# Loading four weight halves instead of two ahead of a loop that runs zero times, in an attention, experts and dense kernel

## The chip, the cores and the metric

The kernel runs on one core of a Trainium2 chip. Its engines are TensorE (PE; its weight loads are PEld), VectorE (DVE), ScalarE (ACT), GpSimd (POOL) and SyncE (SP), which here issues the plain transfers; GpSimd issues the scattered ones. The metric is the device time of one execution in microseconds, as a median over runs.

## The reference

Three stages follow each other, all in float32:

```
q_assign, k_assign = argmax over 16 cluster centroids (normalised q, k)
attn = softmax(where(q_assign == k_assign, q k^T / 8, -1e9)) v      # 2 x 8 heads x 768 x 64
x    = attn as 1536 tokens x 512
e    = argmax(x w_gate); y = gate * sigmoid(x w_og)[e] * relu(x w1[e]) w2[e]   # 8 experts, 512 -> 1024 -> 512
out  = (h * sigmoid(1.702 h)) w_out,  h = y w_in                       # 512 -> 2048 -> 512
```

## The kernel before

**Attention and routing.** 96 score steps run over batch, pair of heads, head and block of 128 queries. At their end the tokens are routed: the vector engine ranks each token within its expert (`route`, L504), and GpSimd scatters the scaled token rows into a buffer in device memory, `xd`, in which every expert has a region of its own (L603). Twelve scatters of 128 rows of 2 KB do it: six for batch 0 in the middle of attention, and the last six (`xd<-xw`) at its very end. `finish_routing` (L627) then counts the tokens of each expert, sorts the experts by count, and works out `trip` (L667), the number of surplus blocks of 128 tokens, of experts that have more tokens than a fixed capacity. Behind it in the code `keep_clock_last(90)` (L746) gives TensorE 90 multiplications of 128x128 whose result nobody reads, so that it isn't idle through this stretch.

**The loop over surplus rows** (L992) runs `trip` times. With these inputs it runs no time at all. All five engines read `trip` (L988) and take the branch past the body. On that path and behind it each engine runs a row of semaphore waits, L992 in the trace: SyncE first waits for every plain transfer that has been issued, and then each engine waits for all scatters, all plain transfers and the count of work done of every other engine. So this point is a meeting of everything.

**The experts.** Then the eight experts run, largest first. Expert `e` has its rows loaded from `xd` (`win_load`, L870; the first one in three pieces, `xr<-xd`), transposed by TensorE (`win_x`, L883) and split into a high part (ACT, L887) and a low part (DVE, L888). The weights come in halves of 512 KB, (expert, quarter of the hidden width, w1 or w2), in the order of the list `order` (L963): w1 of quarter 0, w1 of quarter 1, w2 of quarter 0, w1 of quarter 2, w2 of quarter 1, and so on. `load_half` (L767, transfer at L785) loads one into a tile `raw`; `split_pair` (L794) makes of it the high part (`hi`, ACT, L799) and the low part (`rest`, L802, on DVE or GpSimd). `loads_to(n)` (L967) issues the loads up to number n. The transfers, rows and weights, all stand in SyncE's queue and are issued in its order.

The pool `raw` has four buffers; a second pool, `rawd`, has two. Before the change the first two halves go into `rawd`:

```
load_half(ekeys[n_], half, exps[ekeys[n_][1]], rawd if loaded[0] < 2 else None)
```

`rawd` is also what the loop's body and the dense layer's loads use. The two halves are loaded ahead of the loop (L984); the program that is built from the code has their high and low parts ahead of it too, though the low parts are called for behind it (L1083).

Behind the loop, TensorE first runs 20 more multiplications that nobody reads (`warm(20)`, L1091), then the transposes of the first expert's rows, six more (L1095), and the first products (L895 to L897). The dense layer with its own loads (`dense_load`) follows after the experts, partly interleaved.

Of the kernel before, what the change touches and what calls it, by code (L numbers as in the profile page):

```python
# [45 lines left out]
def attention_moe_ffn(ctx: ExitStack, tc: tile.TileContext, q, k, v, centroids, w_gate, w_og, w1, w2, w_in, w_out, out):  # L46
# [75 lines left out]
    def load_unit(u):  # L122
        b, pr = UNITS[u]
        d = st[u] = {}
        for nm, src in (("q", q), ("k", k), ("v", v)):
            t = ld.tile([128, 2, T, D], F32, name=f"ld_{nm}", tag=f"ld_{nm}")
            nc.sync.dma_start(out=t, in_=src[b, 2 * pr:2 * pr + 2].rearrange("h (p t) d -> p h t d", t=T))
            d[nm] = t
# [10 lines left out]
    def keep_clock_last(n):  # L139

        z = ps_s.tile([128, 2, 512], F32, name="sp", tag="sp")
        for m in range(n):
            nc.tensor.matmul(z[:, m % 2, 0:128], identb, identb, start=True, stop=True)

    def setup_first():
        nc.vector.memset(idle, 0.0)
        keep_clock(7)
        nc.sync.dma_start(out=craw, in_=centroids.rearrange("h c d -> (h c) d"))
        load_unit(0)
        make_identity(nc, ident)  # L150
        nc.vector.tensor_copy(identb, ident)
        ii = one.tile([128, C], I32, name="ii")
        nc.gpsimd.iota(ii, [[-1, C]], base=C, channel_multiplier=0)
        nc.vector.tensor_copy(rev16, ii)
        nc.vector.memset(pen_scale[0:32], 1.0)
        nc.vector.memset(pen_scale[32:64], BIG)
        nc.vector.memset(pen_scale[64:80], BIG)
        nc.vector.memset(pen_bias[0:32], 0.0)
        nc.vector.memset(pen_bias[32:64], -BIG)
        nc.vector.memset(pen_bias[64:80], -BIG)  # L160
# [21 lines left out]
    def setup_blocks(cnorm):  # L182
        pc = ps_a.tile([128, 512], F32, name="pc", tag="po")
        nc.tensor.transpose(pc[:, :128], cnorm.rearrange("p a d -> p (a d)"), ident)
        for r in range(2):
            src = pc[64 * r:64 * r + 64, :128].rearrange("p (h c) -> p h c", h=H)
            hi = cblk[64 * r:64 * r + 64, :, r, :]
            nc.scalar.copy(hi, src)
            nc.vector.tensor_tensor(cblk[64 * r:64 * r + 64, :, 2 + r, :], src, f32(hi), op=ALU.subtract)
# [311 lines left out]
    def sum_logits(b):  # L501
        nc.vector.tensor_reduce(lgp[b], xw[b][:, :, 0:H - 2, D:XW].rearrange("p t h c -> p t c h"), op=ALU.add, axis=AX.X)
# [190 lines left out]
    with tc.manual_schedule():  # L693
        setup_first()
        first = prep_pieces(0)
        load_unit(1)
        cnorm = setup_centroids()
        for n, piece in enumerate(first):
            if n == 1:
                setup_blocks(cnorm)  # L700
            if n == 3:
                keep_clock(8)
            for f in piece:
                f()
        setup_rest()
        emit_scores(0)
        emit_exp(0)
        for i in range(NS + 2):
            nu, r = divmod(i + 3, 12)
            if i == 3 or r == 0 and nu + 2 < len(UNITS):  # L710
                load_unit(nu + 2)
            prepare(i, True)
            if i + 1 < NS:
                emit_scores(i + 1)
            tail = i >= NS - TAIL
            if (tail or i % 3 == 2) and ost:
                ost.popleft()()
            prepare(i)
            if i == 0:
                spots[:] = [(ps_m, "m")]  # L720
            if i >= 14 and i % 4 == 2 and len(fill) < E:
                zero_rows(len(fill))
            if i % (NS // 2) == NS // 2 - 5 and i < NS:
                sum_logits(i // (NS // 2))
            if i == NS // 2 + 13:
                routing.append(route(0))
            for _ in range(2 if tail else 1):
                if av:
                    av.popleft()()
            if 0 <= i - 1 < NS:  # L730
                emit_pt(i - 1)
            n = i - (1 if tail else 2)
            if 0 <= n < NS and steps[n][2] % 3 == 2:
                queue_av(n)
            if i + 1 < NS:
                emit_exp(i + 1)
        advance(stop="weighed")
        while av:
            av.popleft()()
        while ost:  # L740
            ost.popleft()()
        advance()
        routing.append(route(2))
        advance()
        finish_routing()
        keep_clock_last(90)  # L746
    at.close()


    rawd = ctx.enter_context(tc.tile_pool(name="rawd", reuse_waits="tile", bufs=2))  # L750
# [14 lines left out]
    exps = list(experts(lead))  # L765
# [11 lines left out]
    def load_half(key, i, ex, pool=None):  # L777
        d = pairs.setdefault(key, {})
        if ex is None:
            src = pair_of(w_in, w_out, key[2])  # L780
        else:
            src = pair_of(w1[bass.ds(ex, 1)].rearrange("o d f -> (o d) f"), w2[bass.ds(ex, 1)].rearrange("o f d -> (o f) d"), key[2])
        t = (pool or raw).tile([128, 1024], F32, name="raw", tag="raw")
        g = src[i].shape[1]
        nc.sync.dma_start(out=t.rearrange("p (g n) -> p g n", g=g), in_=src[i])  # L785
        d["raw", i] = t
# [172 lines left out]
    ekeys = [("e", e, c) for e in range(E) for c in range(4)]  # L959
    loaded = [0]  # L960
# [6 lines left out]
    def loads_to(n):  # L967

        while loaded[0] < min(n, len(order)):
            n_, half = order[loaded[0]]  # L970
            load_half(ekeys[n_], half, exps[ekeys[n_][1]], rawd if loaded[0] < 2 else None)
            loaded[0] += 1

    xp = cx.enter_context(tc.tile_pool(name="xp", reuse_waits="tile", bufs=2))
# [6 lines left out]


    with tc.manual_schedule():
        loads_to(2)  # L984
        low_parts = [split_pair(ekeys[n_], half, None, nc.vector, True) for n_, half in order[:2]]


# [91 lines left out]

    with tc.manual_schedule():  # L1080
        win_start(0, True)
        loads_to(6)
        for f in low_parts:  # L1083
            f()

        z = ps_h.tile([128, 512], F32, name="ph", tag="ph")

        def warm(n):
            for m in range(n):
                nc.tensor.matmul(z[:, :128], identb, identb, start=True, stop=True)  # L1090
        warm(20)  # L1091
        for r in range(wins[0]["nr"]):
            win_x(wins[0], r)
            if r == wins[0]["nr"] - 1:
                warm(6)  # L1095
        n_, half = order[2]
        split_pair(ekeys[n_], half)
        exps += experts(plan[:, 1:E])
        dense_load(2)
        win_start(1)  # L1100
        loads_to(7)
        G = E * 8
        hq = deque()
        for g in range(G + 2):
            e, c = divmod(g, 8)
            nxt = wins.get(e + 1)
            r = c - (7 - nxt["nr"]) if nxt else 0
            split_low = low = out_low = None
            if g + 3 < len(order):
                n_, half = order[g + 3]  # L1110
                split_low = split_pair(ekeys[n_], half, None, nc.vector if g % 4 == 3 else nc.gpsimd, g % 4 == 3)
                loads_to(g + 7)
            if nxt and 0 <= r < nxt["nr"]:
                win_x(nxt, r)
            if g < G:
                ht, low = win_h(wins[e], ("e", e, c // 2), c % 2, True)
                hq.append((g, ht))
            if g == G + 1:
                dense_in(0)
            if g >= 2:  # L1120
                g0, ht = hq.popleft()
                e0, c0 = divmod(g0, 8)
                win_y(wins[e0], ("e", e0, c0 // 2), c0 % 2, ht, c0 == 0, c0 == 7)
                if c0 == 7:

                    col = e0 and nc.s_assert_within(offs[e0], LEAST + (e0 - 1) * ((NT - LEAST) // (E - 1)), NT, skip_runtime_bounds_check_because="a sum of counts")
                    out_low = win_out(wins[e0], col, True, nc.vector if e0 == E - 1 else None)
            if split_low:
                split_low()
            for f in (low, out_low):  # L1130
                if f:
                    f()
            dense_step(min(5 * e + max(0, c - 2), 40) + 3 * min(max(0, g - 61), 2))
            if g < G:
                if c == 0 and e and e + 1 < E:
                    win_start(e + 1)
                if g == 2:
                    offs = nc.values_load_multi_w_load_instructions(plan[:, E:], engines=[ACT_E, DVE_E, POOL_E], min_val=0, max_val=NT)[1]
# [108 lines left out]
```

## Time and profile before

| | us |
|---|---|
| median of 3 runs (lowest, highest) | 755.31 (752.32, 755.86) |
| profiled execution, its own time | 755.41 |
| its span, first to last instruction | 753.6 |
| TensorE busy | 721.8 (96% of the span) |
| mean granted clock of TensorE | 0.98 of full speed |

All times of day below are microseconds from the start of the span. TensorE is busy nearly throughout, so what a change is worth is looked for where it isn't, or where its clock is at the lower of its two levels; the line PEclk of the page (tenths of full speed, 40 slices of 18.8 us) shows the two places, at the start and near 275 to 297, which is the passage from routing to experts.

### The profile page before, as it was taken

The page shows a single profiled execution, that of the slowest core. Times are in us where ns is not written, and L with a number is a line of the kernel's source. Part 1 is how long each engine was busy: PE and PEld are TensorE (multiplying, and loading weights), DVE is VectorE, ACT ScalarE, POOL GpSimd, SP SyncE. Part 2 cuts the span into 40 slices and gives each one's busy share as a digit, 9 for nine tenths or more (in the row PEclk, how much of TensorE's full clock was granted, in tenths as well). Part 3 has the DMA queues.
Part 4 walks back from the last instruction along what each step waited for, and adds up shares of the span by engine and source line. Part 5 has one row for each costly group of instructions (what it writes and reads, how often), then busy time and mean ns, then how long its engine had stood idle before and what let it go on. Part 6 is the DMA issues. An engine that isn't in the chain of part 4 may idle for free.

```text
span 753.6 us, 12278 instructions
## 1 busy us (share of the span) xinstructions
PE 721.8 (96%) x4314; PEld 635.2 (84%) x4314; DVE 509.5 (68%) x1000; ACT 422.3 (56%) x873; POOL 267.8 (36%) x205
## 2 busy tenths in 40 slices
PE   8999999999899978999999988999999999999996
PEld 5799899898799967999989888777888888888885
DVE  6899999999989982444776666797655556332322
ACT  3787787777778753456767776445434344212120
POOL 4112131120841023666768888232333122020202
PEclk7899999999999987999999999999999999999999
DMA  8756749438160037756756775133534311010101
GB/s 232 158 159 185 209 144 298 117 87 194 54 172 11 1 107 262 264 186 213 252 172 239 242 245 194 56 113 112 58 54 60 75 64 57 0 57 0 57 1 56
DMA packets 66241, 98.23 MB, mean 130 GB/s; under 512 B 9249, under 2 KB 44961, under 8 KB 66177
## 3 DMA queue, kind: packets, MB, share of 16 engines
q1 hardware_dynamic: 63872, 91.12, 42.4%
q0 software_dynamic: 2304, 6.30, 2.2%
q8 instruction: 35, 0.57, 0.3%
q14 instruction: 30, 0.24, 0.1%
HBM read 64.46 MB, written 12.59 MB: 102 GB/s over the span
## 4 chain that ended last, share of the span: by engine, by line
PE 57%; issue 16%; DVE 13%; ACT 5%; POOL 4%; DMA 4%; SPq 1%; POOLq 0%; ACTq 0%; DVEq 0%
PE pt L448 6%; PE po L470 4%; PE ph L1076 4%; PE ph L1075 4%; PE ph L1077 4%; PE sp L432 3%; PE po L471 3%; PE sp L431 3%; PE py L1169 3%; PE py L1168 3%; PE py L1167 3%; ACT w L799 2%; PE pox L487 2%; DVE ptl L453 2%; DVE nm L434 2%
## 5 line engine op out<-in xcount | busy, mean ns | idle before, releaser
L802 POOL TENSOR_TENSOR w<-raw,w 128x1024 fp32r<-128x1024 f32 x47 | 117.1, 2505 | 34.9 <-ACT w L799 19.3
L452 ACT CAST pth<-pt 128x384 fp32r<-128x384 f32 x192 | 83.7, 484 | 43.5 <-PE pt L448 43.4
L453 DVE TENSOR_TENSOR ptl<-pt,pth 128x384 fp32r<-128x384 f32 x192 | 97.6, 546 | 14.3 <-ACT pth L452 13.9
L1152 DVE TENSOR_TENSOR sg<-ph,sg 128x512 f32<-128x512 f32 x48 | 33.2, 691 | 103.5 <-ACT sg L1151 103.1
L434 DVE TENSOR_REDUCE nm<-sp 128x1 f32<-128x768 f32 x96 | 90.9, 947 | 4.3 <-PE sp L432 4.3
L849 POOL TENSOR_TENSOR w<-csq,w 128x512 fp32r<-128x512 f32 x32 | 43.5, 1359 | 139.0 <-ACT w L848 137.2
L440 ACT ACTIVATE P<-sp,nm 128x768 f32<-128x768 f32 x96 | 88.0, 917 | 3.0 <-DVE nm L434 2.8
L1151 ACT ACTIVATE sg<-ph 128x512 f32<-128x512 f32 x48 | 28.7, 598 | 108.7 <-PE ph L1077 105.4
L448 PE MATMUL pt<-ident,P 128*128 128x128 f32 x576 | 80.9, 274 | 2.4 <-DVE ptl L453 2.3
L448 PEld LDWEIGHTS pt<-ident,P 128*128 128x128 f32 x576 | 67.7, 141 | 10.4 <-DVE ptl L453 6.4
L1076 PE MATMUL ph<-ytl,w 128*128 128x512 f32 x192 | 76.1, 396 | 0.0
L1075 PE MATMUL ph<-yth,w 128*128 128x512 f32 x192 | 76.0, 396 | 0.0
L1077 PE MATMUL ph<-yth,w 128*128 128x512 f32 x192 | 75.6, 394 | 0.0
L1168 PE MATMUL py<-w,gh 128*128 128x512 f32 x192 | 75.3, 392 | 0.0
L1169 PE MATMUL py<-w,gl 128*128 128x512 f32 x192 | 75.2, 392 | 0.0
L1167 PE MATMUL py<-w,gh 128*128 128x512 f32 x192 | 75.0, 390 | 0.0
L431 PE MATMUL sp<-X,Q 128*128 128x384 f32 x192 | 73.9, 385 | 0.6 <-DMA X<-Lk 0.6
L799 ACT CAST w<-raw 128x1024 fp32r<-128x1024 f32 x64 | 66.8, 1044 | 6.3 <-DMA raw<-in_moe_w_dram 5.5
L470 PE MATMUL po<-pth,vst 128*128 128x384 f32 x192 | 70.3, 366 | 0.0
L899 PE MATMUL py<-ht,w 128*128 128x480 f32 (+5 forms) x192 | 61.0, 369 | 8.3 <-DVE room L906 5.1
L432 PE MATMUL sp<-Z,Q 80*128 80x384 f32 x192 | 66.5, 346 | 2.1 <-DMA Q<-ohT 2.1
L471 PE MATMUL po<-ptl,vst 128*128 128x384 f32 x192 | 64.9, 338 | 0.0
(240 smaller groups left out, 1676.0 us busy)
## 6 DMA issues: line engine op xcount, KB each, us to landing
raw<-in_moe_w_dram SPq DMA_DIRECT2D x64, 512.0 KB, 3.9
raw<-in_moe_w_in_dram SPq DMA_DIRECT2D x16, 512.0 KB, 4.2
raw<-in_moe_w_out_dram SPq DMA_DIRECT2D x16, 512.0 KB, 4.1
Q<-Hq SPq DMA_DIRECT2D x32, 192.0 KB, 6.0
xd<-zrow SPq DMA_DIRECT2D x8, 768.0 KB, 6.2
ld_q<-in_q_dram SPq DMA_DIRECT2D x8, 384.0 KB, 3.5
ld_k<-in_k_dram SPq DMA_DIRECT2D x8, 384.0 KB, 4.3
ld_v<-in_v_dram SPq DMA_DIRECT2D x8, 384.0 KB, 6.0
```

The lines of the kernel that those rows point to most:

```text
L431: nc.tensor.matmul(sp[:, n, :384], d["Q1"][:, h, cs], d["X"][:, h, ks], start=True, stop=False)
L434: nc.vector.tensor_reduce(nm, sp[:, :, :384], op=ALU.max, axis=AX.XY, negate=True)
L448: nc.tensor.transpose(pt[:, r * 128:(r + 1) * 128], L["P"][:, n, r * 128:(r + 1) * 128], ident)
L453: nc.vector.tensor_tensor(L["ptl"][:, 3 * n:3 * n + 3, qs], src, f32(hi), op=ALU.subtract)
L470: nc.tensor.matmul(hold["o"][:, :384], w, L["pth"][:, kt, :], start=(kt == 0), stop=False)
L802: (eng or nc.gpsimd).tensor_tensor(lo, r, f32(hi), op=ALU.subtract)
L1075: nc.tensor.matmul(ph, wa(key, 0, k, i), yth[:, k, cs], start=(k == 0), stop=False)
L1076: nc.tensor.matmul(ph, wa(key, 0, k, i), ytl[:, k, cs], start=False, stop=False)
L1077: nc.tensor.matmul(ph, wa(key, 1, k, i), yth[:, k, cs], start=False, stop=(k == 3))
L1167: nc.tensor.matmul(po[m], gh[:, ms], wb(key, 0, i), start=first, stop=False)
L1168: nc.tensor.matmul(po[m], gh[:, ms], wb(key, 1, i), start=False, stop=False)
L1169: nc.tensor.matmul(po[m], gl[:, ms], wb(key, 0, i), start=False, stop=last)
```

## The change

Three edits stand in the diff. The dummy multiplications at the end of routing are 75 instead of 90. The first two weight halves go into `raw` like all others, and four instead of two are loaded ahead of the loop, which fills the four buffers. Behind the loop the call for the low parts of the first two stands ahead of `loads_to(6)` instead of behind it; loads 5 and 6 take the buffers that these two low parts read.

```diff
@@ -743,7 +743,7 @@
         finish_routing()
-        keep_clock_last(90)
+        keep_clock_last(75)
     at.close()
@@ -968,7 +968,7 @@
             n_, half = order[loaded[0]]
-            load_half(ekeys[n_], half, exps[ekeys[n_][1]], rawd if loaded[0] < 2 else None)
+            load_half(ekeys[n_], half, exps[ekeys[n_][1]])
             loaded[0] += 1
@@ -981,7 +981,7 @@
     with tc.manual_schedule():
-        loads_to(2)
+        loads_to(4)
         low_parts = [split_pair(ekeys[n_], half, None, nc.vector, True) for n_, half in order[:2]]
@@ -1079,9 +1079,9 @@
         win_start(0, True)
-        loads_to(6)
         for f in low_parts:
             f()
+        loads_to(6)
```

SyncE's queue, just ahead of the reading of `trip` (the signs are those of the difference between the two programs; 128x4x256 is a half of w1, 128x2x512 a half of w2):

```order
 L785 ISA
 L785 DMA raw<-in_moe_w_dram 128x4x256
+L785 ISA
+L785 DMA raw<-in_moe_w_dram 128x2x512
+L785 ISA
+L785 DMA raw<-in_moe_w_dram 128x4x256
 L988 TENSOR_LOAD trip
 L988 ISA x2
```

Loads 3 and 4 now stand ahead of the branch; the same two rows are gone from behind the three loads of the first expert's rows.

The end of that piece once more, of the changed kernel, with the semaphores that each instruction waits for (DMAHW0 to DMAHW7 are those of SyncE's own transfers):

```order
L785 ISA
L785 DMA raw<-in_moe_w_dram 128x2x512 [waits DMAHW1_49]
L785 ISA
L785 DMA raw<-in_moe_w_dram 128x4x256 [waits DMAHW2_49]
L988 TENSOR_LOAD trip [waits DVE_49]
L988 ISA x2
L992 COMPARE_AND_BRANCH
L992 UNCONDITIONAL_BRANCH [waits SP_sequencer_49,DMAHW0_49,DMAHW1_49,DMAHW2_49,DMAHW3_49,DMAHW4_49,DMAHW5_49,DMAHW6_49,DMAHW7_49]
```

The path that skips the loop waits for all eight of SyncE's transfer semaphores, now with four loads of weights under them, before with two.

VectorE before, around the reading of `trip`:

```order
L666 TENSOR_REDUCE tot<-over 1x1
L667 CAST trip<-tot 1x1
L802 TENSOR_TENSOR w_4166<-raw,w_4166 128x1024
L802 TENSOR_TENSOR w_4168<-raw,w_4168 128x1024
L988 TENSOR_LOAD trip
L992 COMPARE_AND_BRANCH
```

and VectorE of the changed kernel, at the loop's end:

```order
L992 COMPARE_AND_BRANCH
L992 UNCONDITIONAL_BRANCH
L802 TENSOR_TENSOR w_4155<-raw,w_4155 128x1024
L802 TENSOR_TENSOR w_4157<-raw,w_4157 128x1024
L888 TENSOR_TENSOR t<-pxt,t 128x4x128 x2
L888 TENSOR_TENSOR t<-pxt,t 128x4x64
L923 SCALAR_TENSOR_TENSOR ht<-ph,ht 128x320 x3
```

The two low parts have moved from ahead of the branch to behind the loop, directly ahead of the low parts of the first expert's rows. ScalarE's two casts that they need (L799) have moved with them, to directly ahead of its first L887.

## Rows read from the trace of the kernel before

**Rows 1.** The page: its head, and the granted clock in 40 slices.

```profile
span 753.6 us, 12278 instructions
...
PEclk7899999999999987999999999999999999999999
```

**Rows 2.** All waits of TensorE, 294 to 480: in total, times, longest.

```profile
PE py L899 <- DVE room L906: 5.1, 4, 1.5
PE py L899 <- DVE ht L923: 3.1, 4, 1.1
PE ph L899 <- DVE ht L923: 1.5, 1, 1.5
```

**Rows 3.** The chain that ended last, 282 to 296: start, length, what.

```profile
282.42 4.01 DMA xd<-xw,di
286.44 0.02 SPq L992
...
287.46 0.35 SPq L870
...
288.03 3.74 DMA xr<-xd
```

**Rows 4.** Waits of SyncE's queue, 265 to 320.

```profile
SPq L988 <- DVE trip L667: 7.2, 1, 7.2
...
SPq L992 <- DMA xd<-xw,di: 1.1, 1, 1.1
```

**Rows 5.** Timeline of SyncE's transfer issues: start, length, what, count.

```profile
275.11 1.01 SPq L785 DMA_DIRECT2D raw<-in_moe_w_dram  x2
...
289.51 2.15 SPq L785 DMA_DIRECT2D raw<-in_moe_w_dram  x4
```

**Rows 6.** Timeline of TensorE, 274 to 300; brackets: idle before it, releaser.

```profile
278.13 7.66 PE L143 MATMUL sp<-identb 128*128 128x128 bf16 x90
287.94 1.29 PE L1090 MATMUL ph<-identb 128*128 128x128 bf16 x20 [2.15 <-issue]
290.48 1.11 PE L883 MATMUL pxt<-ident,xr 128*128 128x128 f32 x4 [1.25 <-DMA xr<-xd]
```

**Rows 7.** Stretches: length, PE busy (count), PEclk, DMA share, GB/s.

```profile
283.00:284.00 1.00, 1.00 (x17) 0.82 0.62 238
290.00:291.00 1.00, 0.52 (x3) 0.59 0.93 283
...
297.00:298.00 1.00, 1.00 (x8) 1.00 1.08 364
```

**Rows 8.** Timeline of GpSimd: the first of the six last scatters.

```profile
275.27 1.08 POOL L603 DMA_INDIRECT xd<-xw,di  x1 [39.11 <-ACT xw L600]
```

**Rows 9.** DMA, 276 to 279.5: queues (packets, MB, share), scatters issued (count, us to landing).

```profile
q1 hardware_dynamic: 769, 0.77, 76.9%
...
xd<-xw,di POOLq DMA_INDIRECT x3, 6.3
```

**Rows 10.** DMA, 280.5 to 283: the scatters' queue.

```profile
q0 software_dynamic: 291, 0.97, 95.5%
```

**Rows 11.** DMA, 194 to 194.5: a scatter of batch 0, nothing beside it.

```profile
xd<-xs,di POOLq DMA_INDIRECT x1, 2.9
```

**Rows 12.** DMA, 289 to 294: SyncE's queue, with four weight loads in it.

```profile
q1 hardware_dynamic: 953, 1.45, 94.0%
```

**Rows 13.** Half a microsecond: length, PEclk, DMA share, GB/s.

```profile
284.50:285.00 0.50, 1.00 0.28 107
```

**Rows 14.** Timelines of ScalarE, then VectorE: casts and low parts around the loop.

```profile
281.73 1.04 ACT L799 CAST w<-raw 128x1024 fp32r<-128x1024 f32 x1 [0.89 <-issue]
291.63 0.59 ACT L887 CAST t<-pxt 128x512 fp32r<-128x512 f32 x1 [8.86 <-PE pxt L883]
...
283.33 2.36 DVE L802 TENSOR_TENSOR w<-raw,w 128x1024 fp32r<-128x1024 f32 x2
292.24 0.69 DVE L888 TENSOR_TENSOR t<-pxt,t 128x512 fp32r<-128x512 f32 x1 [6.55 <-DMA xr<-xd]
```

## The prediction

> **What bounds the kernel now.** I read the page's clock line first: TensorE's clock is below full speed only at the start and in the slices around 275 to 300, which the change touches [rows 1]. Then TensorE's waits in the experts' stage: from 294 to 480 it waits 9.7 us in all, each time for an addition of VectorE behind products (L906, L923), never for weights [rows 2]. So getting weights earlier saves nothing there by itself. What can move is the passage before it: the chain of waits runs through the last scatter (282.42, landed 286.43), SyncE's row of waits at L992 (286.44 to 287.46), the load of the first expert's rows, and the transposes [rows 3]. SyncE's own waits agree: it waits for `trip` for 7.2 us, then 1.1 us for the scatters [rows 4]. TensorE is ready earlier: its 90 dummies end at 278.13 + 7.66 = 285.79, VectorE's low parts at 283.33 + 2.36 = 285.69 [rows 6, 14]. The meeting at L992 is thus set by transfers, with 0.6 us to spare for the engines.
>
> In this passage the granted clock is at its lower level (1.2 GHz) twice. It rises to 2.4 GHz at about 283.4, during the dummies; falls at about 290.2, after TensorE had been idle for 2.15 and 1.25 us around the `warm` products; and is back at about 297.0, while the first expert runs [rows 6, 7]. So TensorE's first 6.5 us on the experts, from 290.48, go at half speed.
>
> **The change, part by part.**
>
> *75 dummies instead of 90.* At full clock `warm(20)` gives a step of (1.29 - 0.22)/19 = 0.056 us [rows 6] (0.22 us, my estimate, for the last one to run through). Fifteen fewer let TensorE arrive at L992 0.84 us earlier, at about 285.0. It was not the last to arrive, so this gains 0 here. The cover is the scatters' landing at 286.43. Its price is a longer idle stretch, which can only touch the clock, and that is low from 290.2 anyway.
>
> *Casts and low parts behind the loop.* Two casts of 1.04 us on ScalarE and two low parts of 1.18 us on VectorE [rows 14] leave a place where they cost nothing and come to one where both engines were idle: ScalarE until 291.63, VectorE until 292.24 (6.55 us of waiting). Let T be when the queues run on, about 287.6 before (TensorE's next instruction starts at 287.94). The casts end at T + 2.1 and the second low part, which starts behind the second cast, at T + 3.4, that is 291.0 on the old clock of events. The first row casts come at T + 4.0, the row low parts at T + 4.6. Cost 0; if the rows came 1.2 us sooner after T, the low parts would be late by the excess. What is queued behind them: L887 and L888, for which the first product waits. Loads 5 and 6 now wait for these low parts at the head of SyncE's queue, 0.3 and 1.1 us beyond the times at which they would have gone out; behind them stand the reading of `plan`, the dense loads and the next expert's rows. All of it is needed only after loads 3 and 4, which are there already, and TensorE showed no wait on any weight. Cost 0.
>
> *Loads 3 and 4 ahead of the loop.* Two issues of 0.5 us each go in front of SyncE's reading of `trip`, at 276.1 to 277.1 [rows 5]; SyncE waited there until 283.4, so the issue is free. Behind them nothing is issued before the branch. The transfers are not free: 2 x 0.524 MB travel while the six scatters should, and L992 waits for both. This is the term that counts.
>
> The scatters' bytes are 6 x 128 x 2 KB = 1.57 MB. The first is issued at 275.27 [rows 8]; alone, such a scatter lands 2.9 us after its issue [rows 11]. Here it does not: between 276 and 279.5 SyncE's queue moves 0.77 MB at a share of 76.9% and the scatters' queue nothing, and the scatters then under way take 6.3 us [rows 9]. From 280.5 to 283 the scatters' queue has 95.5% and moves 0.97 MB [rows 10]. So as long as weights are queued, the scatters stand back.
>
> The sum, if that goes on: 4 x 0.524 = 2.10 MB of weights, of which 0.77 are through at 279.5. The other 1.33 MB at the rate of four queued loads, 1.45 MB in 5 us = 0.29 MB/us [rows 12], take 4.6 us, to 284.1. The scatters, 1.57 MB at 0.97/2.5 = 0.388 MB/us [rows 10], take 4.05 us, to 288.1. Before, their bytes were through at about 285.0 [rows 13], and the landing came 1.4 us later, at 286.43. So everything from L992 on is later by 3.1 us.
>
> Bounds: the least is the two loads at the best rate, 1.05/0.388 = 2.7 us, less the room that stood free, 23% of 3.5 us [rows 9] and 72% of 0.5 us [rows 13], 1.2 us in all: 1.5 us. The most is the two loads at the slow rate of rows 9 (0.22 MB/us): 4.8 us. I take 3.1, since rows 9 show the scatters standing back and not sharing.
>
> The Trainium skill (DMA: Bandwidth & Descriptors, Queues, rings and completion order) says that each DMA engine alternates between the queues it has work for, packet by packet. By that the scatters would flow beside the weights, and the sum would be nearer to the lower bound, 1.5 us. Rows 9 disagree for 3.5 us on end, so I don't follow it here.
>
> *What 3.1 us costs.* TensorE starts the transposes at 293.6 instead of 290.48. Both times lie in the stretch at half clock, which ended at 297.0. Time lost at half clock is half the work: if the rise stays at 297.0, 3.1 x 0.5 = 1.55 us are lost. Nothing gives them back: no wait of TensorE later is one on weights.
>
> Sum: 0 + 0 + 1.55. Against the profiled execution's own 755.41 that is 757.0; that execution lies 0.1 above the median of 755.31, so no correction is made.
>
> **The rivals.** "No change" means within 0.5% of 755.31, that is 751.5 to 759.1, about what a measurement can tell.
>
> *A. Forecast:* scatters behind weights, half of it paid: 757.0; with the bounds 1.5 and 4.8 us it runs from 756.2 to 757.8. Chance 0.50.
>
> *B. The queues share, or the weights use idle room:* the meeting moves by 0 to 1.5 us and half is paid: 755.4 to 756.2. In an execution in which the clock stays low through all the dummies, 90 of them would last to 278.13 + 90 x 0.112 = 288.2, and be the last at L992 by 1.8 us; 75 would end at 286.5. Then the change takes away up to 1.7 us, to 754. For it: 23% of room in rows 9. Against it: not a packet of the scatters in there. Chance 0.29.
>
> *C. Slower for certain: the clock goes with TensorE.* If the rise to 2.4 GHz does not stand still but follows the start of TensorE's work, or fails to come at 297 because TensorE has only been at it since 293.6, the delay is paid in full or more. The price: in full 3.1 us (758.5), at the upper bound 4.8 us (760.2); if the lower level lasts for another stretch like that from 290.2 to 297.0, 6.8 us at half speed, 1.55 + 3.4 = 4.95 (760.4). It decides from 3.8 us on, so either the transfers reach beyond 4 us or the second stretch comes. For it: both falls of the clock followed idle TensorE, and the idle time before `warm` grows from 2.15 us to 2.15 + 0.84 + 3.1 = 6.1. Against it: the first rise came 5.2 us after the start of the dummies (278.13 to 283.4), and TensorE would be busy again before 297 with `warm` and transposes. Chance 0.18, most of it beyond 759.1.
>
> *D. Faster:* the clock does not fall at all in the passage, or for less long. The stretch from 290.48 to 297.0 at half speed is worth 6.5/2 = 3.3 us: 752.1, and the lowest run, 752.32, may be such a one. Nothing in the change makes it likelier, as TensorE is idle for longer. Chance 0.03.
>
> **How the numbers follow.** Likeliest is A: 757.0. B reaches down to about 754, and D is left out below, as is most of what a single execution's clock can give; above, C reaches to 760.4. The range of 753.8 to 760.4 leaves out D and a little at each end. Slower by over 0.5% takes C beyond 759.1, 0.14, and 0.02 from a long tail of A. Faster takes D and what noise does to B, 0.03. Within 0.5%: 0.81. A's own range is 756.2 to 757.8.
>
> **What would show it right or wrong.** Right: SyncE issues four loads from 275.1 to 277.1; the scatters' queue moves nothing until about 283 or 284; SyncE's longest wait at L992 grows from 1.1 us to about 4; its first L870 comes at about 290.5 instead of 287.46; TensorE's idle time before `warm` is about 6 us; the transposes start at about 293.6; the clock is up again near 297; from there on everything is as before. Step by step: scatter packets between 277 and 281 would refute the standing back (B); a first L870 before 288.5 would refute the price; ScalarE's L887 or VectorE's L888 waiting for L799 or L802 instead of for TensorE would refute that the moved casts are hidden; low clock beyond 299 is C. The prediction is wrong altogether if the experts' stage behind 300 changes its length by more than 1 us, since it rests on weights never being waited for there.

## The result, and the profile after

The changed kernel takes 758.89 us (median of 7 runs, 756.23 to 759.82), the kernel before, on the same chip, 754.74 us (7 runs, 752.32 to 755.86). The ratio is 1.0052, with an interval of 1.0030 to 1.0074: 4.15 us by the medians. The forecast of 757.0 was 1.9 us short of that. The time lies inside the whole range of 753.8 to 760.4, but above the 756.2 to 757.8 of the likeliest case, A.

The profiled execution took 759.82 us. The head of its page and the clock line, beside [rows 1]:

```profile
span 758.0 us, 12240 instructions
...
PEclk8999999999999996999999999999999999999999
```

The span is 4.4 us longer. The clock is again low only at the start and in the slice that holds the change, so the place to look at is the same. Two executions don't reach this place at the same moment. So I count from SyncE's first weight issue ahead of the loop (L785). Its timeline, beside [rows 5] and the L870 of [rows 3]:

```profile
275.19 2.21 SPq L785 DMA_DIRECT2D raw<-in_moe_w_dram  x4
...
291.07 1.70 SPq L870 DMA_DIRECT2D xr<-xd  x3
...
292.98 1.00 SPq L785 DMA_DIRECT2D raw<-in_moe_w_dram  x2
```

All four loads are issued at once. From the first of them to the first load of the expert's rows (L870) it is 291.07 - 275.19 = 15.88 us; before it was 287.46 - 275.11 = 12.35. The meeting at L992 therefore lets SyncE go 3.5 us later. SyncE's waits in the same passage (total, times, longest), beside [rows 4]:

```profile
SPq L992 <- SPq L992: 4.3, 2, 3.6
```

The wait at L992 has grown from 1.1 to 3.6 us, and it is no longer put down to the scatters. "SPq L992 <- SPq L992" names only SyncE's own instruction. The trace's records of this wait, one for each semaphore, say what it was: SyncE passed the third load's semaphore at 285.47 and the fourth's at 289.05, and then the seventeen waits that were left, none of which had to wait any more, up to 290.66. So the fourth weight half ended the meeting; the last scatter had landed at 288.5. The view of the issues around 277 gives the time from that load's issue to its landing:

```profile
raw<-in_moe_w_dram SPq DMA_DIRECT2D x1, 512.0 KB, 12.0
```

Before, the same records show the scatters' wait as the long one, 1066 ns up to 286.46. It stands in the second half of the row of waits: from its end to the first L870 it was 1.0 us, and from the end of the fourth load's wait it is 2.0 us. So the 3.5 us have two parts. The last transfer lands 2.5 us later (13.84 us after the first load, before 11.32), and 1.0 us is the rest of the row of waits, which before was worked off while the scatters were still on their way.

The chain that ended last (start, length, what), beside [rows 3]:

```profile
289.45 0.04 SPq L992
289.49 0.47 issue
...
291.07 0.35 SPq L870
...
292.18 4.67 DMA xr<-xd
```

Behind the meeting stands the third piece of the expert's rows, 4.67 us after its issue. Before, the chain went through the second piece (the 3.74 us of [rows 3]); the third took 3.8 us and was not waited for. TensorE's timeline, beside [rows 6] (start, length, what; in brackets its idle time before and the releaser):

```profile
278.20 5.95 PE L143 MATMUL sp<-identb 128*128 128x128 bf16 x75
290.16 2.32 PE L1090 MATMUL ph<-identb 128*128 128x128 bf16 x20 [6.01 <-SPq L992]
293.65 1.97 PE L883 MATMUL pxt<-ident,xr 128*128 128x128 f32 x8 [1.18 <-DMA xr<-xd]
296.89 0.69 PE L883 MATMUL pxt<-ident,xr 64*128 64x64 f32 x4 [1.27 <-DMA xr<-xd]
...
298.09 0.62 PE L895 MATMUL ph<-t,w 128*128 128x320 f32 x1
```

TensorE is idle for 6.0 us before `warm`, for 1.18 us before the first transposes and for 1.27 us before the last ones. The first product of the experts (L895) starts at 298.09, 22.90 us after the first load. Before, it started at 294.06, 18.95 us after:

```profile
294.06 0.62 PE L895 MATMUL ph<-t,w 128*128 128x320 f32 x1
```

Stretches of TensorE (length, busy time and count, granted clock, DMA share, GB/s), beside [rows 7]:

```profile
286.00:288.00 2.00, 0.00 (x0) 1.00 0.64 254
288.00:289.00 1.00, 0.00 (x0) 0.71 0.04 14
...
301.00:302.00 1.00, 1.00 (x6) 0.50 0.94 258
302.00:303.00 1.00, 1.00 (x9) 0.96 0.70 217
```

The clock falls to 1.2 GHz at about 288.4, while TensorE is idle, and is back at 2.4 GHz at about 302.0. Before, the lower level held from 290.2 to 297.0. That makes 13.6 us instead of 6.8 in these two executions, and the rise came later with TensorE's work.

DMA, three stretches of the changed kernel, beside [rows 9] and [rows 10] (queue: packets, MB, share of 16 engines; q0 is the scatters', q1 SyncE's). First 276 to 279:

```profile
q1 hardware_dynamic: 636, 0.63, 71.0%
```

Then 281 to 282:

```profile
q1 hardware_dynamic: 132, 0.24, 79.4%
q0 software_dynamic: 12, 0.03, 7.2%
```

Then 282 to 283:

```profile
q0 software_dynamic: 52, 0.21, 50.7%
q1 hardware_dynamic: 95, 0.19, 50.3%
```

Until 279 the scatters' queue moves nothing; before, until 279.5. From 279 to 282 it has a small part of the engines, 27%, 32% and 7% in the three microseconds, and from 282 to 286 about half, 47 to 63%. So the scatters stand back for longer than 279, but the two don't come one behind the other.

The moved casts on ScalarE and low parts on VectorE, beside [rows 14]. ScalarE:

```profile
290.08 1.99 ACT L799 CAST w<-raw 128x1024 fp32r<-128x1024 f32 x2 [10.11 <-SPq L992]
...
294.80 0.59 ACT L887 CAST t<-pxt 128x512 fp32r<-128x512 f32 x1 [2.73 <-PE pxt L883]
```

VectorE:

```profile
291.15 2.36 DVE L802 TENSOR_TENSOR w<-raw,w 128x1024 fp32r<-128x1024 f32 x2 [7.72 <-ACT w L799]
...
295.42 0.69 DVE L888 TENSOR_TENSOR t<-pxt,t 128x512 fp32r<-128x512 f32 x1 [1.91 <-ACT t L887]
```

The casts of weights are done at 292.07, and ScalarE then waits 2.73 us for TensorE's transposes before L887; the low parts are done at 293.51. Neither is waited for. TensorE's waits from 296 to 484 (total, times, longest), beside [rows 2]:

```profile
PE py L899 <- DVE room L906: 4.9, 4, 1.4
PE py L899 <- DVE ht L923: 2.3, 3, 1.1
PE ph L899 <- DVE ht L923: 1.5, 1, 1.5
PE pxt L883 <- DMA xr<-xd: 1.3, 1, 1.3
```

These are the waits of before, 8.7 instead of 9.7 us, and one new one, for the row piece. None is for weights, so I see nothing that having loads 3 and 4 earlier gave back.

### The profile page after: what moved, and what is told of

It reads as the page before. It is cut to its first block, busy times and chain, and to the rows that moved or that the text cites. A ratio compares the mean times of both kernels' runs of the same rounds, so it can differ in the third digit from the quotient of the medians.

```text
span 758.0 us, 12240 instructions
## 1 busy us (share of the span) xinstructions
PE 722.0 (95%) x4299; PEld 635.9 (84%) x4299; DVE 507.2 (67%) x1000; ACT 422.3 (56%) x873; POOL 267.1 (35%) x205
## 4 chain that ended last, share of the span: by engine, by line
PE 28%; issue 16%; DVE 9%; ACT 5%; POOL 3%; DMA 1%; POOLq 0%; SPq 0%; ACTq 0%; DVEq 0%
PE ph L1077 3%; PE ph L1076 3%; PE ph L1075 3%; PE py L1169 3%; PE py L1168 3%; PE py L1167 3%; ACT w L799 2%; PE ph L895 1%; DVE w L802 1%; PE py L899 1%; PE ph L896 1%; PE ph L899 1%; DVE ct L837 1%; PE ph L897 1%; PE py L895 1%
## 5 line engine op out<-in xcount | busy, mean ns | idle before, releaser
L799 ACT CAST w<-raw 128x1024 fp32r<-128x1024 f32 x64 | 66.6, 1044 | 12.1 <-SPq L992 10.1
```

## The experiments

Theory M (meeting): the time is lost because L992 waits for loads 3 and 4, and nothing later repays it. Rival Q (queues of work): the casts and low parts behind the loop hold something up. Rival K (clock): the 15 missing dummies do it, through TensorE's clock. Each version was timed in five rounds against the kernel before on the same chip. "Meeting" is the first L870 less the first L785, as above, in the one profiled execution of each; two more profiles with two loads ahead (two_ahead_again and warm_42, below) gave 11.81 and 12.54.

| version | loads ahead | ratio to before, 95% interval | meeting, us |
|---|---|---|---|
| before | 2 | 1 | 12.35 |
| after | 4 | 1.0052 [1.0030, 1.0074] | 15.88 |
| two_ahead | 2 | 1.0001 [0.9982, 1.0020] | 12.15 |
| three_ahead | 3 | 1.0016 [0.9997, 1.0036] | 13.69 |
| four_rest_before | 4 | 1.0062 [1.0043, 1.0081] | 15.95 |
| dummies_75 | 2 | 0.9985 [0.9967, 1.0003] | 12.51 |
| one_ahead | 1 | 1.0032 [1.0015, 1.0050] | 11.32 |
| one_ahead_later | 1 | 1.0014 [0.9993, 1.0035] | 11.31 |

**two_ahead**: the changed kernel, with two loads ahead as before.

```diff
-        loads_to(4)
+        loads_to(2)
```

> The changed kernel with two loads ahead of the loop instead of four, all else as changed. Theory M (the meeting at L992 waits for loads 3 and 4): the first L870 goes back to about 287.5, SyncE's wait at L992 to about 1 us, and the time to the kernel before, within 0.7 us of it. Rival Q (the casts and low parts behind the loop, and loads 5 and 6 behind them, cost the time): stays about 4 us above the kernel before, with L887, L888 or L883 late. Rival K (15 fewer dummies cost the time through the clock): stays 1.7 to 4 us above.

Measured: 754.78 us (751.19 to 756.52), before 754.37. The same edit in a later set of runs (two_ahead_again) gave 754.52 us and 0.9999 [0.9983, 1.0015].

> The changed kernel with two loads ahead, once more, beside one_ahead_later on the same chip, as its measure. Within 0.7 us of the kernel before, as the first time.

SyncE's timeline of two_ahead:

```profile
273.78 1.05 SPq L785 DMA_DIRECT2D raw<-in_moe_w_dram  x2
...
285.93 1.71 SPq L870 DMA_DIRECT2D xr<-xd  x3
```

Its chain at the meeting:

```profile
281.07 3.84 DMA xd<-xw,di
284.91 0.02 SPq L992
```

The scatters end the meeting again, 3.84 us after the last issue, as in [rows 3], and the whole loss is gone. The moved casts and low parts and the 75 dummies are all still in this kernel, so Q and K fall by this run alone, as causes of the 4 us.

**three_ahead**: three loads.

```diff
-        loads_to(4)
+        loads_to(3)
```

> The changed kernel with three loads ahead of the loop. Theory M: one load of 0.52 MB less in flight at about 0.29 to 0.39 MB/us brings the meeting 1.3 to 1.8 us forward against the changed kernel, first L870 at about 289.3; time 1.5 to 2.5 us above the kernel before. Rivals Q and K: as the changed kernel, about 4 us above.

Measured: 755.56 us (754.12 to 758.10). SyncE's timeline:

```profile
273.29 1.64 SPq L785 DMA_DIRECT2D raw<-in_moe_w_dram  x3
...
286.98 1.71 SPq L870 DMA_DIRECT2D xr<-xd  x3
```

The chain at its meeting:

```profile
280.57 5.38 DMA xd<-xw,di
285.95 0.02 SPq L992
```

One load more delays the last scatter's landing from 3.84 to 5.38 us after its issue, and the meeting by 13.69 - 12.15 = 1.5 us. The scatters still end it. The time grows by 0.16%, 1.2 us, with an interval that just includes nothing; 1.5 to 2.5 us were expected. In order of loads, then, 2, 3 and 4 give a meeting at 12.2, 13.7 and 15.9 us. Each load has its price, 1.5 and 2.2 us, and the fourth costs more than the 1.3 to 1.8 expected for it: the last landing moves by only 1.2 us there (12.66 to 13.84 us after the first load), and 1.0 us is the row of waits, which now stands behind the load that comes last.

**four_rest_before**: the kernel before, with four loads ahead and nothing else changed.

```diff
-        loads_to(2)
+        loads_to(4)
```

> The kernel before with four loads ahead of the loop and nothing else changed: the first two in their own pool, their casts and low parts ahead of the loop, 90 dummies. Theory M: the whole loss is there, 3.5 to 4.5 us above the kernel before, first L870 at about 291. Rivals Q and K: no loss, within 0.7 us.

Measured: 758.86 us (756.84 to 760.24). SyncE's timeline:

```profile
274.43 2.27 SPq L785 DMA_DIRECT2D raw<-in_moe_w_dram  x4
...
290.38 1.71 SPq L870 DMA_DIRECT2D xr<-xd  x3
```

Its waits at L992, and TensorE's last transposes:

```profile
SPq L992 <- SPq L992: 4.4, 2, 3.6
```

```profile
295.83 0.68 PE L883 MATMUL pxt<-ident,xr 64*128 64x64 f32 x4 [0.73 <-DMA xr<-xd]
```

The two loads alone bring the whole loss, 4.5 us by the medians, the same wait of 3.6 us, and again a small wait for the row piece. With two_ahead this shows M from both sides: with the loads taken out of the change the loss is gone, and with them put alone into the kernel before it is there.

**dummies_75**: the kernel before, with 75 dummies.

```diff
-        keep_clock_last(90)
+        keep_clock_last(75)
```

> The kernel before with 75 dummies instead of 90 and nothing else changed. Theory M: TensorE is earlier at a meeting that the scatters set, so 0, within 0.7 us. Rival K: 1.7 to 4 us above the kernel before, with a longer stretch at half clock.

Measured: 753.45 us (751.41 to 755.45); the interval includes no difference. SyncE's timeline:

```profile
272.36 1.02 SPq L785 DMA_DIRECT2D raw<-in_moe_w_dram  x2
...
284.87 1.71 SPq L870 DMA_DIRECT2D xr<-xd  x3
```

The meeting is where it was, 12.51 us; TensorE waited longer there (3.93 us instead of 2.15). In the profiled execution the clock was at its lower level from 285.7 to 296.0, longer than the 6.8 us of before, and still the time was no longer. K falls by this run too.

If each load ahead delays the meeting, fewer might be better than before. **one_ahead** is the changed kernel with one load ahead; the second half's low part goes behind the first window of rows.

```diff
-        loads_to(4)
-        low_parts = [split_pair(ekeys[n_], half, None, nc.vector, True) for n_, half in order[:2]]
+        loads_to(1)
+        low_parts = [split_pair(ekeys[n_], half, None, nc.vector, True) for n_, half in order[:1]]
...
-        loads_to(6)
+        loads_to(5)
...
+        n_, half = order[1]
+        split_pair(ekeys[n_], half, None, nc.vector)
+        loads_to(6)
```

> The changed kernel with one load ahead of the loop; the second half is loaded behind the first expert's rows and split behind their casts. Theory M: with 0.52 MB instead of 1.05 MB in flight beside the scatters the last scatter lands nearer to the 2.9 us of one alone, about 1 us sooner, first L870 11.0 to 11.5 us after the first load's issue (12.4 in the kernel before); time 0.3 to 1 us below the kernel with two ahead, if nothing waits for the second half. Rival (the scatters' landing does not depend on the weights beside them): first L870 stays at 12.2 to 12.5 us and the time within 0.5 us of two ahead.

Measured: 757.29 us (one execution of 2441.94 us stands far apart from all others). SyncE's timeline:

```profile
273.27 0.41 SPq L785 DMA_DIRECT2D raw<-in_moe_w_dram  x1
...
284.59 2.05 SPq L870 DMA_DIRECT2D xr<-xd  x3
...
286.84 8.72 SPq L785 DMA_DIRECT2D raw<-in_moe_w_dram  x5
...
298.94 0.89 SPq L813 DMA_DIRECT2D raw<-in_moe_w_in_dram  x2
```

TensorE, at the second expert:

```profile
307.22 0.72 PE L883 MATMUL pxt<-ident,xr 128*128 128x128 f32 x4 [3.56 <-DMA xr<-xd]
```

The meeting comes 1.0 us sooner, and the kernel is slower all the same. Five issues stretch over 8.72 us, because the last of them, at the head of SyncE's queue, waits for the buffer of the second half: 3.7 us until that half has landed and 2.2 us more for its low part. Behind it stand the dense loads (L813) and the second expert's rows, and for the rows TensorE waits 3.56 us.

**one_ahead_later** takes that wait away: load 6 goes out with load 7, behind the second expert's rows.

```diff
         n_, half = order[1]
         split_pair(ekeys[n_], half, None, nc.vector)
-        loads_to(6)
```

> One load ahead of the loop, as in one_ahead, but the sixth load, which has to wait there for the second half's low part and held SyncE's queue, issued later, with the seventh, behind the second expert's rows. If the 2.5 us that one_ahead lost are that held queue (TensorE waited 3.6 us for the second expert's rows), they go, and what is left is the meeting about 1 us sooner: 0.3 to 1.2 us below the kernel with two ahead and 75 dummies. If one_ahead lost for want of the second half itself, it stays 2 to 3 us above the kernel before.

Measured: 754.46 us (753.32 to 758.60), before 754.07. SyncE's timeline:

```profile
272.72 0.41 SPq L785 DMA_DIRECT2D raw<-in_moe_w_dram  x1
...
284.03 2.24 SPq L870 DMA_DIRECT2D xr<-xd  x3
...
286.48 2.14 SPq L785 DMA_DIRECT2D raw<-in_moe_w_dram  x4
...
291.99 0.89 SPq L813 DMA_DIRECT2D raw<-in_moe_w_in_dram  x2
```

The queue runs on: L813 starts 19.3 us after the first load instead of 25.7, and from the first product to the end of the span it is 460.7 us, in one_ahead 464.7. By the medians the kernel is 0.4 us above its kernel before, one_ahead 2.5 us (757.29 against 754.83); the intervals overlap, so that the queue cost about 2 us over all executions is likely and not settled. The 1.0 us gained at the meeting does not show in the time: beside two_ahead_again on the same chip the median is 0.1 us lower, where 0.3 to 1.2 us were expected. Beside the profile of two_ahead, 0.8 us at the meeting are 0.5 us at the first product (18.3 us after the first load against 18.8), as TensorE waits 1.99 us for the first rows instead of 0.72. Behind that product the clock stays at its lower level for 5.4 us instead of 4.6.

**warm_42** and **one_ahead_warm_42** ask what the half clock behind the meeting is worth: 42 products in `warm` instead of 20, in the kernel before and in one_ahead.

```diff
-        warm(20)
+        warm(42)
```

> The kernel before with 42 dummies behind the loop instead of 20, so that TensorE is busy until the first rows land, at about 290.4. If the idle time of 1.25 us before the transposes has a part in the fall of the clock, the stretch at half clock over the first expert goes or is shorter in part of the executions, 0.5 to 3 us faster. If the fall hangs on the idle time at the meeting alone, no change, within 0.7 us; if the dummies run at half clock they last past the rows' landing and cost up to 2 us.

> One load ahead of the loop and 42 dummies behind it, both as in the two runs beside it. The two effects are of different things and should add: the time is that of one_ahead plus the difference that warm_42 shows against the kernel before, within 1 us.

Measured: warm_42 754.33 us, 0.9994 [0.9972, 1.0016]; one_ahead_warm_42 757.91 us, 1.0036 [1.0017, 1.0055], like one_ahead. TensorE's timeline of warm_42:

```profile
289.72 2.52 PE L1090 MATMUL ph<-identb 128*128 128x128 bf16 x42 [2.24 <-issue]
292.54 0.66 PE L883 MATMUL pxt<-ident,xr 128*128 128x128 f32 x4 [0.30 <-DMA xr<-xd]
```

Its clock in the first expert's products:

```profile
294.00:296.00 2.00, 1.84 (x15) 1.00 0.88 272
```

The longer `warm` leaves 0.30 us of idle time before the first transposes, and in this execution the clock stays at full speed. From the first product to the second expert's transposes it still takes 12.07 us, before 12.16: TensorE now waits 0.37 us for a low part and 0.62 us for the second expert's rows. The median doesn't move. One profile shows one execution only, and I can't say in how many others the clock stayed up; so this experiment doesn't settle the clock's price. one_ahead_warm_42 was expected within 1 us of 756.8 and came out 1.1 us above that. No version is faster than the kernel before beyond its interval.

## Why the prediction came out as it did

The direction, the place and the cause were right; the size of the loss was not, and of that one factor most of all.

**The 75 dummies, 0:** right in the time (two_ahead and dummies_75). The clock itself fell sooner here, at 288.4. The meeting makes most of that idle time: four_rest_before, with all 90, was idle there for 5.45 us, and its clock was low from 287.2 to 300.9, 13.7 us.

**Casts and low parts behind the loop, 0:** right. L887 waited for the transposes and not for L799, and two_ahead, with the parts moved, takes the time of before.

**Loads 3 and 4, the meeting 3.1 us later:** measured 3.5, inside the bounds of 1.5 to 4.8. SyncE's row of four issues, its wait of 3.6 us and TensorE's idle time of 6.0 us are as foretold. But the reason given was partly wrong, and that the size came out so near is luck. "As long as weights are queued, the scatters stand back": they moved nothing until 279, had little of the engines until 282 and about half from then on, and the fourth weight half came last, 12.0 us after its issue, not the scatters. The transfers' part was 2.5 us, not 3.1. The other 1.0 us, the longer rest of the row of waits, was not in the sum: I took it that the scatters would still end the meeting, with only 1.0 us of waits behind theirs. That the transfers' part was still near, I put down to the sum of bytes: L992 waits for the weights as well as the scatters, and with the engines full, the order in which the two are carried alters little in when both are through (no run changed the order of the two queues alone). The Trainium skill (DMA: Bandwidth & Descriptors, Queues, rings and completion order) has an engine alternate between its queues. The trace agrees from 282 on (50.7% and 50.3% from 282 to 283) and not ahead of it. I was wrong to turn that rule into a smaller loss: it tells in which order the bytes are carried, and they are no fewer by it.

**"Half of it paid", 1.55 us:** this is the term that was mis-sized; it measured 4.15 us. I let the end of the half-clock stretch stand still at 297.0, so that a delay inside it cost half. It did not stand still: the stretch ended at 302.0. The parts in the profiled execution, counted from the first load: the meeting 3.5 us, the passage from there to the first product, with the third row piece in it, 22.90 - 18.95 - 3.5 = 0.4 us, and from the first product to the end of the span 459.9 us instead of 459.5, 0.4 us. With the 0.1 us by which the first load itself was later, that is 4.4 us, the difference of the spans. The last part fits the clock, which stayed low for 302.0 - 298.1 = 3.9 us behind the first product instead of 297.0 - 294.1 = 2.9, so 1.0 us more at half speed, 0.5 us by that estimate. That part is not a sure effect of the change: in two_ahead the clock was low until 297.2, 4.6 us behind its first product, and in dummies_75 as long. What both kernels with four loads share is the delay of the first product (22.90 and 22.60 us after the first load, against 18.7 to 19.0 in the profiles with two), paid in full. This is rival C's mechanism, at 0.18; the rows held what spoke for it, since both falls of the clock had followed an idle TensorE, and a delay makes TensorE idle. I should have made it the forecast: 755.4 + 3.1 = 758.5.

**Weights not waited for later:** right. From 296 on nothing but the one row piece is new among the waits.

Rival B (room for the weights beside the scatters) is refuted by the meeting at 15.9 us. Its sign, scatter packets between 277 and 281, did appear from 279 on: that sign was ill chosen, since here the queues shared and the meeting was 3.5 us later all the same.

What stays open: why the third row piece took 0.9 us longer than before (TensorE waited for it 1.27 us here and 0.73 us in four_rest_before), why the first rows took longer in one_ahead_later, and why the stretch of low clock differs so much between executions with two loads ahead.

## What to carry to other kernels

The loop of this kernel runs no times and is still a meeting: all engines and all transfers in flight have to arrive before anything behind it starts, so a load put ahead of it "for free" is paid for in the wait if the transfers there are already the last to arrive. Where a program has such a place, count the bytes of all that it waits for, look which wait will end last and how many waits stand behind that one, and put a load ahead only if something behind waits for it. And before a delay is called half price because it lies in a stretch of low clock, ask whether that stretch stays where it is when TensorE's work moves.

## What the runs showed of the hardware

The first of the scatters moved its first packet 3.7 us after its issue in the changed kernel, 4.3 us in the kernel before, 2.5 us with one load ahead, and 1.8 us with nothing beside it (the scatter of [rows 11]). By this comparison nearly half of the time in which the scatters seemed to stand back is their own start. After that, in the changed kernel, the two queues shared the engines, unevenly until 282 and about evenly from then on. Each load ahead made the last scatter later: 2.85, 3.84, 5.38 and 6.0 us from issue to landing with one, two, three and four loads, against 2.9 us with nothing beside it [rows 11].

Each of these transfers lands in sixteen parts, as the trace's records of its semaphore show, and at the meeting the last part was a straggler: of the fourth load fifteen parts had landed by 287.23 and the sixteenth at 289.03; of the last scatter before, fifteen by 285.1 and the sixteenth at 286.4.

One load that waits for its buffer at the head of SyncE's queue made TensorE wait 3.56 us in one_ahead, though that load itself wasn't needed yet: what was needed stood behind it.
